# Squares of k summed on GpSimd, sums of q and decoded words in PSUM, a third weight piece and a fifth held group inside S

## The chip, the cores and the metric

One core of a Trainium2 chip runs the whole program. The metric is the device time of one launch in microseconds. TensorE (PE in the profile) multiplies, VectorE (DVE) and ScalarE (ACT) work element by element, GpSimd (POOL) does the same on SBUF only, SyncE (SP) issues most transfers. Each engine runs its own list of instructions in order and waits on semaphores.

## The reference

Three steps follow one another on 6080 tokens. The first is a channel attention: q and k (6080 x 256) are divided by the norm of each column over all tokens, and their product over the tokens is a 256 x 256 matrix S.

```
qn = q / (norm(q, axis=1) + 1e-6);  kn = k / (norm(k, axis=1) + 1e-6)
a  = softmax(kn^T @ qn / tau);      x = (v @ a)
g  = max(0.01 h, h), h = x @ w_in;  x = g @ w_out             # moe
g  = h where h >= 1, 0 where h <= -1, else (h + 1)^2 / 4      # moe2, h = x @ w2_in
out = g @ w2_out
```

All inputs are float32 in value; the four weight matrices (256 x 2048 and 2048 x 256) arrive as 64-bit words, so each weight has two 32-bit halves that the kernel has to join.

## The kernel before

**The stage S.** The tokens come in 15 groups: groups 0 to 3 with two tokens to a partition (256 KB for q, 256 KB for k), groups 4 to 12 with four (512 KB each), group 13 with two, group 14 with two on 96 partitions. Buffers for q and for k turn in rings of six. For a group TensorE adds k^T q into two PSUM banks, `s_ps[0]` and `s_ps[1]`, one for each half of k's columns (L358); a four-token group gives eight products, and each product leaves two rows in the profile. The last `HELD` groups get only the first bank's products in the loop; those for the second bank are kept in a list and issued later by `s_held`: `PRE` (one) right behind the loop, some behind the norm products, the rest behind the first transposes.

**The norms.** ScalarE squares q and k of each group (L376, L379), and VectorE adds the squares to `accq` and `acck`, both in SBUF (L382, L384; folded and finished at L389 and L387). When all groups are in, TensorE sums them over the partitions with a matrix of ones (`nq`, L425; `nk`, L429), ScalarE takes roots (L426, L430), VectorE inverts them (L433 to L436), scales S (L449), takes the maximum (L450), ScalarE the exponential (L451), TensorE turns it (`et_ps`, L456), and a product with the first weights follows (`wps`, L469).

**Weight pieces.** The weights come in 32 pieces of 512 KB (`raw`, three buffers, L144). One piece costs ScalarE a magnitude (L184, `a<-raw`) and VectorE three single-input operations (L197, L199, L206) and three with two inputs (L202, L210, and the last sum L214, L217 or L233); pieces that are used in two parts (high and low) also cost a cast on ScalarE (L224, L241) and a difference on VectorE (L221, L237). This work is a generator, `preparation`, which `pump` and `step` advance from fixed places in the program; ScalarE's parts wait in the list `later` until `flush`, the differences in the list `behind`. `LOAD_AT` names the groups behind whose loads a piece is loaded while S runs. Before, two pieces are decoded inside S and the third around the norms.

**What follows.** The expert layers run as quads (layer, pair of token blocks, slice of the hidden size). The first pair's eight quads, (0, 0, j), use the products wx = (attention times w_in): ScalarE scales them out of PSUM (L721, L519), casts the high part (L722, L524) and VectorE subtracts for the low part (L728 for the second half of j = 0, L527 for each later j). TensorE needs both parts for `ph` (L340, L342). The order of these operations is written out by hand: a list of events with times that only sort them (`PLAN0`, `PUMP`, `FLUSH`, `SUMS`, `HIGHS`, `LOWS`). `SUMS` places four VectorE sums of token blocks for the next pair (L704, `xs`).

## Time and profile before

| | before |
|---|---|
| median of 3 runs (lowest to highest) | 1048.63 us (1048.36 to 1048.72) |
| the profiled execution, its own time | 1048.5 us |
| its span in the trace | 1046.6 us |
| TensorE busy | 1039.6 us (99%) |
| VectorE busy | 815.9 us (78%) |
| ScalarE busy | 835.8 us (80%) |
| GpSimd busy | 20.5 us (2%) |

The profile describes one execution. Times in its rows count from the span's start; the profiled execution's own time is 1.9 us longer than the span, and 0.1 us below the median. A busy share is a mean over stages: TensorE at 99% says that little of the span is left to gain, but its ends are modelled, and rows that stand further apart than their neighbours show where it waited. What ended such a wait stands in brackets behind a row, with the idle time before it.

### The profile page before, as it was taken

The numbers are of one execution on the slowest core, as the hardware profiler recorded it, in microseconds if no ns is written. First come the engines' busy times: TensorE is split into PE (matmuls) and PEld (weight loads), VectorE is DVE, ScalarE is ACT, GpSimd is POOL, SyncE is SP. The second block draws the span as 40 slices with busy tenths as digits, with TensorE's granted clock in tenths as the row PEclk, the third lists the DMA queues.
The fourth block names the chain that finished last, engine by engine and source line by source line (L and its number), as shares of the span: only waits on it lengthen the run. The fifth ranks groups of instructions, "written<-read, shape, count | busy, mean of one in ns | idle before, by whom it ended". The sixth has DMA issues, their size and how long they took to land.

```text
span 1046.6 us, 13454 instructions
## 1 busy us (share of the span) xinstructions
PE 1039.6 (99%) x4656; PEld 868.9 (83%) x4656; DVE 815.9 (78%) x1369; ACT 835.8 (80%) x1436; POOL 20.5 (2%) x36
## 2 busy tenths in 40 slices
PE   9999999999999999999999999999999999999998
PEld 8878888888888888888888888888888888888887
DVE  6999967788787878775557878779778878878765
ACT  6677777777777787777678888888888888888886
POOL 0001100000000000000000000000000000000000
PEclk9999999999999999999999999999999999999999
DMA  9754566468668669557346346446436444543641
GB/s 356 262 191 145 196 227 219 136 214 294 220 208 299 214 215 326 199 190 240 129 155 238 117 166 199 159 139 218 155 123 203 157 162 170 184 150 127 206 140 65
DMA packets 50996, 201.82 MB, mean 193 GB/s; under 512 B 5552, under 2 KB 6576, under 8 KB 50928
## 3 DMA queue, kind: packets, MB, share of 16 engines
q1 hardware_dynamic: 46752, 186.54, 51.0%
q0 software_dynamic: 3888, 14.16, 4.4%
q8 instruction: 37, 0.61, 0.2%
q10 hardware_dynamic: 288, 0.26, 0.1%
q14 instruction: 31, 0.25, 0.1%
HBM read 163.32 MB, written 37.62 MB: 192 GB/s over the span
## 4 chain that ended last, share of the span: by engine, by line
PE 96%; DVE 1%; DMA 1%; issue 0%; ACT 0%; SPq 0%; DVEq 0%
PE acc L342 33%; PE acc L340 16%; PE pX L342 15%; PE pW L342 8%; PE pX L340 8%; PE pW L340 4%; PE pY L342 4%; PE s_ps L358 3%; PE ph L342 2%; PE pY L340 2%; PE ph L340 1%; DMA k<-in_k_dram 1%; PE wps L342 0%; PE wps L469 0%; DVE gl L673 0%
## 5 line engine op out<-in xcount | busy, mean ns | idle before, releaser
L673 DVE TENSOR_TENSOR gl<-c,gh 128x512 fp32r<-128x512 f32 (+1 forms) x384 | 261.1, 680 | 69.8 <-ACT gh L668 69.1
L342 PE MATMUL acc<-gl,l2w 128*128 128x512 f32 (+1 forms) x768 | 297.7, 388 | 0.0
L342 PE MATMUL acc<-gh,l2w 128*128 128x512 f32 (+1 forms) x768 | 297.7, 388 | 0.0
L340 PE MATMUL acc<-gh,l2w 128*128 128x512 f32 (+1 forms) x768 | 297.6, 387 | 0.0
L668 ACT CAST gh<-c 128x512 fp32r<-128x512 f32 (+1 forms) x384 | 234.9, 612 | 5.4 <-DVE c L664 0.8
L342 PE MATMUL pX<-xo,l1w 128*128 128x512 f32 (+1 forms) x704 | 215.6, 387 | 0.0
L342 PEld LDWEIGHTS acc<-gl,l2w 128*128 128x128 f32 x768 | 144.2, 188 | 28.8 <-DVE gl L673 0.2
L342 PEld LDWEIGHTS acc<-gh,l2w 128*128 128x128 f32 x768 | 144.2, 188 | 28.5
L340 PEld LDWEIGHTS acc<-gh,l2w 128*128 128x128 f32 x768 | 144.2, 188 | 28.4
L342 PEld LDWEIGHTS pX<-xo,l1w 128*128 128x128 f32 x704 | 132.2, 188 | 26.2
L655 ACT ACTIVATE u<-c,half 128x512 f32<-128x512 f32 (+1 forms) x144 | 103.8, 721 | 42.4 <-DVE c L641 42.3
L340 PE MATMUL pX<-xo,l1w 128*128 128x512 f32 (+1 forms) x352 | 136.3, 387 | 0.0
L633 ACT COPY s<-pX 128x512 f32<-128x512 f32 (+1 forms) x176 | 101.5, 577 | 30.9 <-PE pX L342 30.9
L658 ACT ACTIVATE u<-u 128x512 f32<-128x512 f32 (+1 forms) x192 | 120.3, 627 | 1.3
L650 ACT ACTIVATE c<-c 128x512 f32<-128x512 f32 (+1 forms) x120 | 75.2, 627 | 56.8 <-DVE c L641 56.5
L342 PE MATMUL pW<-xo,l1w 128*128 128x512 f32 (+1 forms) x352 | 107.8, 387 | 0.0
L641 DVE TENSOR_TENSOR c<-pY,s 128x512 f32<-128x512 f32 (+1 forms) x88 | 60.3, 685 | 60.7 <-PE pY L342 58.7
L664 DVE SCALAR_TENSOR_TENSOR c<-u,c 128x512 f32<-128x512 f32 (+1 forms) x144 | 97.9, 680 | 10.7 <-ACT u L658 10.7
L641 DVE TENSOR_TENSOR c<-pW,s 128x512 f32<-128x512 f32 (+1 forms) x88 | 60.2, 685 | 39.7 <-PE pW L342 28.6
L641 DVE TENSOR_TENSOR c<-pX,s 128x512 f32<-128x512 f32 (+1 forms) x88 | 60.2, 684 | 24.1 <-PE pX L342 20.6
L340 PEld LDWEIGHTS pX<-xo,l1w 128*128 128x128 f32 x352 | 66.1, 188 | 13.1
L342 PEld LDWEIGHTS pW<-xo,l1w 128*128 128x128 f32 x352 | 66.1, 188 | 13.1
(118 smaller groups left out, 1104.3 us busy)
## 6 DMA issues: line engine op xcount, KB each, us to landing
l1w<-l1d SPq DMA_DIRECT2D x80, 896.0 KB, 4.6
l2w<-l2d SPq DMA_DIRECT2D x88, 512.0 KB, 5.2
raw<-in_w_out_dram POOLq DMA_DIRECT2D x14, 512.0 KB, 4.6
l1d<-l1w SPq DMA_DIRECT2D x8, 896.0 KB, 4.3
l1d<-l1s SPq DMA_DIRECT2D x8, 896.0 KB, 4.8
raw<-in_w_in_dram POOLq DMA_DIRECT2D x13, 512.0 KB, 4.4
xr<-in_vT_dram SPq DMA_DIRECT2D x5, 1024.0 KB, 8.4
x<-o SPq DMA_DIRECT2D x20, 256.0 KB, 3.7
```

The source lines that it names most:

```text
L340: nc.tensor.matmul(out=out, lhsT=wh, rhs=mh, start=first, stop=False, skip_group_check=skip)
L342: nc.tensor.matmul(out=out, lhsT=w, rhs=x, start=False, stop=last and w is (wl if late else wh), skip_group_check=skip)
L358: nc.tensor.matmul(out=s_ps[ic], lhsT=kt[:rows, i, ic * P:(ic + 1) * P], rhs=qt[:rows, i, :], start=gi == 0 and i == 0, stop=gi == len(gro ...
L633: A.copy(out=s[i], in_=bank["W" if i == "5" else "X"])
L641: V.tensor_tensor(out=tile_c(r), in0=bank[name], in1=s[i], op=ALU.add)
L650: A.activation(out=c[r], in_=src, func=AF.Prelu, alpha=0.01)
L655: A.activation(out=u[r], in_=source(r), func=AF.Relu, scale=0.5, bias=half[:, 0:1])
L658: A.activation(out=u[r], in_=u[r], func=AF.Square)
L664: V.scalar_tensor_tensor(out=c[r], in0=u[r], scalar=1.0, in1=src, op0=ALU.min, op1=ALU.max)
L668: A.copy(out=g[int(r[0]), int(r[1])][0], in_=c[r])
L673: V.tensor_tensor(out=lo, in0=c[r], in1=hi.bitcast(F32), op=ALU.subtract)
```

## The change

- GpSimd adds the squares of k for groups 2 to 11 into `acck` (`add_k`); VectorE adds those of the last three groups into a new tile `sumk` and then both halves of `acck` to it.
- The sums of q, `accq`, now lie in two PSUM banks and VectorE adds half a group at a time (`add_q`); at group 12 they go over into `sumq` in SBUF.
- The magnitudes and the masked words of the first three pieces lie in PSUM (`psum_words`), and the banks of the norms are taken later (`norm_banks`).
- `LOAD_AT` goes from groups 1 and 5 to groups 3, 6 and 9, so that three pieces are loaded inside S; the fourth goes ahead of the first block of v. A piece may be decoded from the group behind its load on. Group 4 has an extra pump ahead of its squares, and pumping goes on through group 12.
- Five groups are held instead of four; ten held products stand behind the norm products instead of six, five are left behind the first transposes as before.
- Three generator steps around the norms are rearranged, and the four sums of token blocks for the second pair go to later quads.

**The end of S, VectorE.** Before, the sums end with folds and four short adds, and the third piece starts behind them; `rq` (L433) is the first operation of the norms.

```order
L384 TENSOR_TENSOR accq<-accq,sq 128x1024
L389 TENSOR_TENSOR accq<-accq 128x512
L384 TENSOR_TENSOR acck<-acck,sq 128x1024
L389 TENSOR_TENSOR acck<-acck 128x512
L387 TENSOR_TENSOR accq<-accq,sq 128x512
L387 TENSOR_TENSOR acck<-acck,sq 128x512
L387 TENSOR_TENSOR accq<-accq,sq 96x512
L387 TENSOR_TENSOR acck<-acck,sq 96x512
L197 TENSOR_SCALAR a<-a 128x512
L199 TENSOR_SCALAR a<-a 128x512
L433 TENSOR_SCALAR rq<-rq 128x256
```

The same place now, from the third piece's masked words on; ahead of these rows stand its L210, L212 and L215 and the two adds of group 11's squares of q.

```order
L219 TENSOR_SCALAR a<-a 128x512
L223 SCALAR_TENSOR_TENSOR raw<-raw,a 128x512
L375 TENSOR_TENSOR sumq<-accq,sq 128x512
L375 TENSOR_TENSOR sumq<-accq,sumq 128x512
L375 TENSOR_TENSOR sumq<-sumq,sq 128x512
L246 TENSOR_TENSOR a<-a,raw 128x512
L375 TENSOR_TENSOR sumk<-sq 128x512
L375 TENSOR_TENSOR sumq<-sumq,sq 128x512
L375 TENSOR_TENSOR sumk<-sumk,sq 128x512
L375 TENSOR_TENSOR sumk<-sumk,acck 128x512 x2
L375 TENSOR_TENSOR sumq<-sumq,sq 96x512
L375 TENSOR_TENSOR sumk<-sumk,sq 96x512
```

The whole third piece now stands among the last sums and ahead of the last add to `sumq`. ScalarE's list at the same place, before (377, 379, 393 to 407 are the tiles of groups 12, 13 and 14; 417 is the third piece):

```order
L379 ACTIVATE sq_385<-q_377 128x1024
L379 ACTIVATE sq_389<-k_379 128x1024
L379 ACTIVATE sq_399<-q_393 128x512
L379 ACTIVATE sq_402<-k_395 128x512
L379 ACTIVATE sq_411<-q_405 96x512
L379 ACTIVATE sq_414<-k_407 96x512
L184 ACTIVATE a_429<-raw_417 128x512
L426 ACTIVATE rq_432<-nq_161,tiny_125 128x256
```

And now (354, 376, 394 and 413 are the tiles of q of groups 10 to 13; 352 is the third piece):

```order
L424 ACTIVATE sq_366<-k_356 128x1024
L197 ACTIVATE a_371<-raw_352 128x512
L424 ACTIVATE sq_384<-q_376 128x1024
L424 ACTIVATE sq_391<-k_378 128x1024
L424 ACTIVATE sq_402<-q_394 128x1024
L424 ACTIVATE sq_409<-k_396 128x1024
L254 CAST l2w_408<-a_371 128x512
L424 ACTIVATE sq_419<-q_413 128x512
L424 ACTIVATE sq_422<-k_415 128x512
L424 ACTIVATE sq_433<-q_427 96x512
```

The third piece's magnitude moved up behind group 10's square of k, and its cast stands ahead of the squares of groups 13 and 14.

**The first quads, ScalarE**, from the last cast of a token block (`xo`) to the high part of j = 1, before:

```order
L414 CAST xo<-xr 128x512
L721 ACTIVATE w_455<-wps_523,sums 128x256
L722 CAST wx<-w_455 128x256
L184 ACTIVATE a<-raw 128x512
L519 ACTIVATE w_549<-wps_458,sums 128x256
L519 ACTIVATE w_549<-wps_551,sums 128x256
L524 CAST wx<-w_549 128x512
```

And now:

```order
L450 CAST xo<-xr 128x512
L197 ACTIVATE a<-raw 128x512
L237 CAST w1i<-a 128x512
L197 ACTIVATE a<-raw 128x512
L760 ACTIVATE w_479<-wps_549,sums 128x256
L761 CAST wx<-w_479 128x256
L558 ACTIVATE w_572<-wps_482,sums 128x256
L558 ACTIVATE w_572<-wps_574,sums 128x256
L563 CAST wx<-w_572 128x512
```

Two magnitudes and a cast of the fourth piece stand ahead of the scaling of wx. VectorE between the low part of j = 0's second half (L728) and that of j = 1 (L527), before:

```order
L202 SCALAR_TENSOR_TENSOR a<-raw,a 128x512
L728 TENSOR_TENSOR wx<-w_455,wx 128x256
L206 TENSOR_SCALAR e<-a 128x512
L210 SCALAR_TENSOR_TENSOR raw<-raw,e 128x512
L217 TENSOR_TENSOR a<-a,raw 128x512
L197 TENSOR_SCALAR a<-a 128x512
L199 TENSOR_SCALAR a<-a 128x512
L527 TENSOR_TENSOR wx<-w_549,wx 128x512
```

And now (L767 and L566 are the same two low parts):

```order
L210 TENSOR_SCALAR a<-a 128x512
L767 TENSOR_TENSOR wx<-w_479,wx 128x256
L212 TENSOR_SCALAR a<-a 128x512
L234 TENSOR_TENSOR w1i<-a,w1i 128x512
L215 SCALAR_TENSOR_TENSOR a<-raw,a 128x512
L219 TENSOR_SCALAR e<-a 128x512
L223 SCALAR_TENSOR_TENSOR raw<-raw,e 128x512
L246 TENSOR_TENSOR a<-a,raw 128x512
L566 TENSOR_TENSOR wx<-w_572,wx 128x512
```

Six operations stand between the two low parts where five stood, and four of them read two tensors where two did. The diff:

```diff
@@ -22,7 +22,7 @@
 WARM = 8
-HELD = 4
+HELD = 5
 SMALL = 4
@@ -55,7 +55,7 @@
 
-SUMS = [((1, 4.5), (1, 13.6), (2, 4.5), (2, 13.6)), ((1, 5.2), (1, 8.3), (2, 5.2), (2, 8.3)), ((1, 6.0), (1, 9.7), (2, 6.0), (2, 9.7))]
+SUMS = [((1, 4.5), (1, 13.6), (2, 4.5), (2, 13.6)), ((1, 5.2), (1, 8.3), (2, 5.2), (2, 8.3)), ((3, 2.5), (5, 2.5), (5, 9.7), (7, 2.5))]
 HIGHS = [((3, 3.3), (4, 3.3), (5, 3.3), (7, 3.3), (7, 9.4), (7, 12.4), (8, 0.4)),
@@ -64,7 +64,7 @@
 
-LOAD_AT = (1, 5)
+LOAD_AT = (3, 6, 9)
 TAU_AT = 3
@@ -179,8 +179,21 @@
 
+    def psum_words(i):
+        if i == 2:
+            norm_banks()
+        return ps_h.tile([P, 2, 256], F32, tag="h", name="a").bitcast(U32)
+
+    norms = []
+
+    def norm_banks():
+        if not norms:
+            norms.append(ps_h.tile([P, NB], F32, tag="h", name="nq")[:, :C])
+            norms.append(ps_h.tile([P, NB], F32, tag="h", name="nk")[:, :2 * KC].rearrange("p (c t) -> p c t", c=KC))
+        return norms
+
     def magnitude(i):
-        a = started[i] = dec.tile([P, 2, 256], U32, tag="a", name="a", bufs=2)
+        a = started[i] = psum_words(i) if i < len(LOAD_AT) else dec.tile([P, 2, 256], U32, tag="a", name="a", bufs=2)
         A.activation(out=a.bitcast(F32), in_=raws[i][:, :, :, 1].bitcast(F32), func=AF.Abs)
@@ -202,7 +215,7 @@
 
-        e = dec.tile([P, 2, 256], U32, tag="e", name="e")
+        e = psum_words(0) if i < len(LOAD_AT) else dec.tile([P, 2, 256], U32, tag="e", name="e")
         V.tensor_single_scalar(out=e, in_=a, scalar=0xFF800000, op=ALU.bitwise_and)
@@ -249,7 +262,7 @@
                 yield 100
-            while not s_done and (i >= len(raws) or loaded_at[i] + 1 > group[0]):
+            while not s_done and (i >= len(raws) or loaded_at[i] > group[0]):
                 yield 100
@@ -342,14 +355,14 @@
 
-    accs = [ep.tile([P, CPG, C], F32, tag=f"acc{nm}", name=f"acc{nm}", bufs=1) for nm in "qk"]
+    accq = [ps_a.tile([P, NB], F32, tag="acc", name="accq").rearrange("p (i c) -> p i c", c=C) for _ in range(2)]
+    acck = ep.tile([P, CPG, C], F32, tag="acck", name="acck", bufs=1)
+    sumq, sumk = (ep.tile([P, 2, C], F32, tag=f"sum{nm}", name=f"sum{nm}", bufs=1) for nm in "qk")
     s_ps = [ps_a.tile([P, NB], F32, tag="acc", name="s_ps")[:, :C] for _ in range(KC)]
...
 
-    nq = ps_h.tile([P, NB], F32, tag="h", name="nq")[:, :C]
-    nk = ps_h.tile([P, NB], F32, tag="h", name="nk")[:, :2 * KC].rearrange("p (c t) -> p c t", c=KC)
     tiles = []
@@ -357,6 +370,34 @@
                              start=gi == 0 and i == 0, stop=gi == len(groups) - 1 and i == s - 1)
+
+    def add(o, x, y):
+        V.tensor_add(out=o, in0=x, in1=y)
+
+    def add_q(gi, sq, rows):
+        if gi < SMALL:
+            add(accq[gi - 2], accq[gi - 2], sq[:, 0:2, :])
+        elif gi < FOLD - 1:
+            for i in range(2):
+                add(accq[i], accq[i], sq[:, 2 * i:2 * i + 2, :])
+        elif gi < FOLD:
+            add(sumq, accq[0], sq[:, 0:2, :])
+            add(sumq, accq[1], sumq)
+            add(sumq, sumq, sq[:, 2:4, :])
+        else:
+            add(sumq[:rows], sumq[:rows], sq[:rows, 0:2, :])
+
+    def add_k(gi, sq, rows):
+        if gi < FOLD - 1:
+            a = acck[:, 2 * gi - 4:2 * gi - 2, :] if gi < SMALL else acck
+            G.tensor_tensor(out=a, in0=a, in1=sq[:, 0:2, :] if gi < SMALL else sq, op=ALU.add)
+        elif gi < FOLD:
+            add(sumk, sq[:, 0:2, :], sq[:, 2:4, :])
+        else:
+            add(sumk[:rows], sumk[:rows], sq[:rows, 0:2, :])
+        if gi == FOLD:
+            for i in range(2):
+                add(sumk, sumk, acck[:, 2 * i:2 * i + 2, :])
 
@@ -371,31 +412,26 @@
             s_matmuls(1, gi)
-        for t, a in ((qt, accs[0]), (kt, accs[1])):
+        if gi == LOAD_AT[0] + 1:
+            pump(0.1)
+            flush()
+            pump(2.4)
+        for t in tl:
             if gi < 2:
-                A.activation(out=a[:, 2 * gi:2 * gi + 2, :], in_=t[:, :s, :], func=AF.Square)
+                A.activation(out=accq[gi] if t is qt else acck[:, 2 * gi:2 * gi + 2, :], in_=t[:, :s, :], func=AF.Square)
             else:
...
                 A.activation(out=sq[:rows, :s, :], in_=t[:rows, :s, :], func=AF.Square)
-                if gi < SMALL:
-                    h = slice(2 * gi - 4, 2 * gi - 2)
-                    V.tensor_add(out=a[:, h, :], in0=a[:, h, :], in1=sq[:, 0:2, :])
-                elif gi < FOLD:
-                    V.tensor_add(out=a, in0=a, in1=sq)
-                else:
-                    for i in range(0, s, 2):
-                        V.tensor_add(out=a[:rows, 0:2, :], in0=a[:rows, 0:2, :], in1=sq[:rows, i:i + 2, :])
-            if gi == FOLD - 1:
-                V.tensor_add(out=a[:, 0:2, :], in0=a[:, 0:2, :], in1=a[:, 2:4, :])
+                add_q(gi, sq, rows) if t is qt else add_k(gi, sq, rows)
             flush()
-            if gi < len(groups) - 4:
+            if gi < FOLD:
                 pump(S_PUMP[gi > 7])
...
             load_pieces(len(raws) + 1, nc.sync)
-    load_pieces(3, nc.sync)
+    load_pieces(4, nc.sync)
     xr = load_x(0, 0, nc.sync)
@@ -417,24 +453,27 @@
 
-    step(1)
     flush()
     s_held(PRE)
+    nq, nk = norm_banks()
     rq = ep.tile([P, C], F32, tag="rq", name="rq", bufs=1)
     for i in range(2):
-        nc.tensor.matmul(out=nq, lhsT=ones, rhs=accs[0][:, i, :], start=i == 0, stop=i == 1)
+        nc.tensor.matmul(out=nq, lhsT=ones, rhs=sumq[:, i, :], start=i == 0, stop=i == 1)
     A.activation(out=rq, in_=nq, func=AF.Sqrt, bias=tiny[:, 0:1])
...
         for i in range(2):
-            nc.tensor.matmul(out=nk[:, c], lhsT=accs[1][:, i, c * P:(c + 1) * P], rhs=ones[:, :2], start=i == 0, stop=i == 1)
+            nc.tensor.matmul(out=nk[:, c], lhsT=sumk[:, i, c * P:(c + 1) * P], rhs=ones[:, :2], start=i == 0, stop=i == 1)
     A.activation(out=rk, in_=nk[:, :, 0], func=AF.Sqrt, bias=tiny[:, 0:1])
     A.activation(out=dummy, in_=tiny, func=AF.Exp)
-    step(2)
+    while behind:
+        behind.pop(0)()
+    step(1)
+    flush()
     V.tensor_scalar_add(out=rq, in0=rq, scalar1=1e-6)
...
     V.reciprocal(out=rk, in_=rk)
-    s_held(6)
+    s_held(10)
 
...
     wx = {}

```

## Rows read from the trace of the kernel before

**Rows 1.** The page, part 1: busy us (share of span) xinstructions.
```profile
PE 1039.6 (99%) x4656; PEld 868.9 (83%) x4656; DVE 815.9 (78%) x1369; ACT 835.8 (80%) x1436; POOL 20.5 (2%) x36
```

**Rows 2.** TensorE's timeline, S to the transposes: start, us, operation, idle before.
```profile
4.57 4.29 PE L358 MATMUL s_ps<-q,k 128*128 128x256 f32 x16
...
13.45 30.03 PE L358 MATMUL s_ps<-q,k 128*128 128x256 f32 x138 [0.22 <-DMA k<-in_k_dram]
43.31 1.02 PE L425 MATMUL nq<-accq,ones 128*128 128x256 f32 x4
...
44.99 2.84 PE L358 MATMUL s_ps<-q,k 128*128 128x256 f32 x12
49.05 0.41 PE L456 MATMUL et_ps<-ident,e 128*128 128x128 f32 x2 [1.22 <-ACT e L451]
```

**Rows 3.** Windows, TensorE alone: stretch, busy (rows), clock, DMA share, GB/s.
```profile
13.45:43.30 29.85, 29.85 (x138) 1.00 1.03 390
```

**Rows 4.** ScalarE's timeline in S.
```profile
22.50 1.06 ACT L379 ACTIVATE sq<-k 128x1024 f32<-128x1024 f32 x1 [0.23 <-DMA k<-in_k_dram]
23.47 0.67 ACT L184 ACTIVATE a<-raw 128x512 f32<-128x512 f32 x1
...
32.92 1.06 ACT L379 ACTIVATE sq<-q 128x1024 f32<-128x1024 f32 x1 [0.22 <-DMA q<-in_q_dram]
...
41.67 0.68 ACT L184 ACTIVATE a<-raw 128x512 f32<-128x512 f32 x1 [0.41 <-DMA raw<-in_w_out_dram]
```

**Rows 5.** VectorE's groups up to 60 us by shape: count | busy, mean ns.
```profile
L384 DVE TENSOR_TENSOR accq<-accq,sq 128x1024 f32<-128x1024 f32 x9 | 11.0, 1225 | 0.1
...
L199 DVE TENSOR_SCALAR a<-a 128x512 uint32<-128x512 uint32 x5 | 2.1, 427 | 0.2
...
L492 DVE TENSOR_SCALAR w<-wps,sums 128x256 f32<-128x256 f32 x1 | 0.5, 483 | 0.0
...
L433 DVE TENSOR_SCALAR rq<-rq 128x256 f32<-128x256 f32 x1 | 0.3, 293 | 0.7 <-ACT rq L426 0.7
```

**Rows 6.** VectorE's timeline, the last sums.
```profile
41.48 0.68 DVE L387 TENSOR_TENSOR acck<-acck,sq 128x512 f32<-128x512 f32 x1
42.08 0.68 DVE L387 TENSOR_TENSOR accq<-accq,sq 96x512 f32<-96x512 f32 x1
```

**Rows 7.** VectorE's timeline around the first quads.
```profile
49.36 0.69 DVE L210 SCALAR_TENSOR_TENSOR raw<-raw,e 128x512 f32<-128x512 uint32 x1
50.09 0.69 DVE L233 TENSOR_TENSOR a<-a,raw 128x512 f32<-128x512 f32 x1
...
54.08 0.17 DVE L462 RECIPROCAL sums<-sums 128x1 f32<-128x1 f32 x1
...
57.35 0.42 DVE L728 TENSOR_TENSOR wx<-w,wx 128x256 fp32r<-128x256 f32 x1
...
60.27 0.68 DVE L527 TENSOR_TENSOR wx<-w,wx 128x512 fp32r<-128x512 f32 x1
```

**Rows 8.** ScalarE's timeline around the first quads.
```profile
55.45 0.47 ACT L721 ACTIVATE w<-wps,sums 128x256 f32<-128x256 f32 x1 [0.80 <-PE wps L469]
55.95 0.41 ACT L722 CAST wx<-w 128x256 fp32r<-128x256 f32 x1
56.26 0.67 ACT L184 ACTIVATE a<-raw 128x512 f32<-128x512 f32 x1
56.84 0.46 ACT L519 ACTIVATE w<-wps,sums 128x256 f32<-128x256 f32 x1
```

**Rows 9.** TensorE's weight loads, the first of j = 1 for wx.
```profile
61.01 0.19 PEld L342 LDWEIGHTS ph<-xo,wx 128*128 128x128 f32 x1
```

**Rows 10.** TensorE's timeline, the first products of j = 2.
```profile
73.34 0.39 PE L340 MATMUL ph<-xo,wx 128*128 128x512 f32 x1
74.00 0.50 PE L342 MATMUL ph<-xo,wx 128*128 128x512 f32 x1 [0.27 <-DVE wx L527]
```

**Rows 11.** GpSimd's groups up to 3 us.
```profile
masks.py:199 POOL TENSOR_SCALAR_AFFINE_SELECT ident<-ident 128x128 f32<-128x128 f32 x1 | 0.3, 287 | 0.1
```

## The prediction

> **What bounds the kernel now.** I read the page's busy shares first: TensorE has rows over 99% of the span [rows 1], so only stretches where its rows stand apart can give time back. Its timeline over S shows them. The 138 rows from 13.45 follow one another without a gap, 30.03 / 138 = 0.218 us each, up to the norm product `nq` at 43.31; then 12 rows of held products start at 44.99, and the transposes at 49.05 had TensorE idle for 1.22 us, waiting for the exponential [rows 2]. The windows add that the DMA engines are full in the same stretch, share 1.03 at 390 GB/s [rows 3]: S is close to two limits at once. VectorE's list shows a third: its last sums run at 41.48 and 42.08 behind one another without a pause [rows 6], so the sum of q is ready just before `nq` starts. The change touches all three, and the question is which ends last.
>
> **The change part by part.** The profiled execution took 1048.5 us, 0.1 less than the median; I sum against it.
>
> *Loads.* The piece behind group 1 goes behind group 3, still ahead of group 4. The bytes ahead of group 4's k stay the same, so with full DMA engines TensorE's start on it at 13.45, which waited for that k [rows 2], stays: groups 2 and 3 come earlier, and the pause only moves. Value 0. The third piece, 512 KB, now goes ahead of group 10 instead of behind group 14. A four-token load of q or k is 512 KB too, so every load behind it lands one place later: group 10's k where group 11's q landed, at whose landing ScalarE squared it, 32.92; and group 14's k, the last of the same set of bytes, where the third piece landed, at 41.67 less the start of its reader, 41.65 [rows 4].
>
> *Held products.* Four products, eight rows, leave the stream before `nq`: 130 rows from 13.45 would end at 41.7. But the last six (two products of group 14 and the `PRE` one) wait for the landing at 41.65: 41.8 + 6 x 0.218 = 43.1. So TensorE could start `nq` at 43.1 against 43.31. Behind it stand now 20 rows instead of 12. From `nq` to the first held row pass 44.99 - 43.31 = 1.68 us [rows 2], 20 rows take 4.35, so the transposes come 6.03 us behind `nq`; the norm chain alone needed 49.05 - 43.31 = 5.74. The 1.22 us idle is filled, and TensorE itself is late next.
>
> *The sums, where I expect the end to be set.* `nq` waits for the last add to `sumq`, and VectorE's list puts the whole third piece and the adds of `sumk` ahead of it. Group 10's square of k starts at 32.92; the magnitude of the third piece stands behind it, 23.47 - 22.50 = 0.97 later, and takes 0.67 [rows 4]: 34.6. From there VectorE has no pause. An operation that needs the one before it starts 50.09 - 49.36 = 0.73 behind it [rows 7]; one that doesn't, 42.08 - 41.48 = 0.60 [rows 6]. From the first masked operation (L210) to the sum L246 are ten such steps, five of each kind: 5 x 0.73 + 5 x 0.60 = 6.65, so L246 starts at 41.25 and ends at 41.95. On it ScalarE's cast (L254) waits, with the squares of groups 13 and 14 queued behind: 0.58 to the next instruction (56.84 - 56.26 [rows 8]) and 0.67 for each square (the magnitude of the same 512 columns) puts group 13's q at 43.25 and its k at 43.95. VectorE adds them at 43.3 and 44.0, both halves of `acck` at 44.7 and 45.45, the last squares of q at 46.05, done at 46.75. So `nq` starts at 46.8, the transposes at 52.85, 3.8 us later than before, and TensorE is idle 3.7 us ahead of `nq`. **+3.8.**
>
> Ends of that term: I take 0.73 for the three single-input operations on PSUM, which the trace shows only in SBUF, at 0.43 for 512 columns; on PSUM 256 columns took 0.483, against 0.293 in SBUF for 256 [rows 5]. At the SBUF price the three steps shrink by 0.27 each, 0.8 in all; if each of the nine PSUM operations on this path cost another 0.1, it is 0.9 more. So +3.0 to +4.7.
>
> By the Trainium skill, "VectorE: DVE Perf Modes", section "Why PSUM operands drop a tier", any PSUM operand takes a float32 single-input operation from two elements a cycle to one. The 256-column pair agrees; by the rule the sum stands as taken, by the SBUF row it would be 1052.3.
>
> *GpSimd's adds* run beside all this if one of 1024 columns takes less than the loads of a group, 1.05 MB at the 390 GB/s of [rows 3], 2.7 us. The trace has none. Below: VectorE's 1.225 for the same add; above: GpSimd's only row that reads data, 0.287 for 128 columns and one input [rows 11], times eight is 2.3, and twice that for two inputs 4.6. I take 2.3, the plain multiple of its own row. Group 11's k lands two places behind group 10's, at 32.9 + 2.6 or 2.7, its square takes 1.06 [rows 4] and the add 2.3: near 39, long before VectorE wants it at 44.7. Cost 0; I price the other end below. The Trainium skill, "GPSIMD Engine Reference", section 3.1, gives 4497 ns for 2048 columns, so by estimate 2.25 here, and the sum would be the same.
>
> *VectorE's adds of q at half a group each* cost 2 x 0.60 where one of k and one of q cost 2.4 before [rows 5]; up to group 9 they lie in its slack. Cost 0, bound by the tail already summed.
>
> *The first quads.* The fourth piece now stands where the third stood. Everything here is relative to the transposes. VectorE's sum of the fourth piece follows the reciprocal at 54.08 [rows 7]: two two-input operations, so it ends near 54.2 + 0.73 + 0.69 = 55.6. Its cast on ScalarE waits for that, and behind the cast a second magnitude and only then the scaling of wx, 2 x 0.58 later: 56.8, where it stood at 55.45 [rows 8]. Its cast ends at 56.8 + 0.50 + 0.41 = 57.7, so L767 starts 0.35 to 0.4 later than L728's 57.35. From there to the low part of j = 1 VectorE took 60.27 - 57.35 = 2.92 [rows 7]; one single-input operation (0.43 [rows 5]) leaves this stretch, two with two inputs (0.60 to 0.73) come: +0.9. So this low part ends 1.3 later, and TensorE's load of it stood at 61.01 [rows 9], directly behind its end at 60.95: no cover. **+1.3**, between 0.3 (a faster piece) and 1.5.
>
> *Later quads.* VectorE is then about one piece, six operations, ahead, and two of the four token sums leave the stretch before j = 2. There TensorE waited for a late low part: its rows stand 0.66 apart, 0.27 of it idle, and the second takes 0.11 longer [rows 10]. That goes: **-0.5**, between the idle alone and the whole, -0.3 to -0.8. The four sums, 0.6 each, come back in quads 3 to 7, where VectorE by then has no backlog; cost 0, at most 1.
>
> Sum: 1048.5 + 3.8 + 1.3 - 0.5 = 1053.1; with the 0.1 to the median, 1053.2. The likeliest case's own range, all low ends and all high ends a little drawn in: 1050.8 to 1054.6.
>
> **The rivals.**
>
> *The tail is covered (not slower).* If the last add to `sumq` starts by 42.4 instead of 46.05, `nq` goes at 43.1, the transposes at 49.1, and 1.3 - 0.5 remain: 1049.4. The place is the third piece's L210, the price 1 us for each us, and the point of decision is `nq` at 44.6, from where it is over 1050.7. For it: VectorE has less to do in S as a whole. Against it: the list puts 18 operations behind group 10's k, and nothing in it can pass another.
>
> *Also the loads give way (faster).* Without the wait for group 14 and without the late low part, TensorE alone sets the pace: `nq` at 41.75, transposes at 47.8, 1.25 early, and -0.5: 1046.8. Against it: the DMA share of 1.03 and the bytes counted above.
>
> *GpSimd late.* At 4.6 an add, eight of them from 14.5 (group 4's k at 13.45 and its square, 1.06) end at 51.3, `nq` follows two steps of 0.73, one of 0.60 and an end later at about 53.5, 6.7 behind my forecast: 1059.8. It decides from (44.7 - 14.5) / 8 = 3.8 us an add.
>
> *TensorE's clock.* The granted clock is 1.00 in every row here, idle 1.22 us included. At the span's start, after a long idle, 16 rows of S took 4.29 instead of 3.48 [rows 2]. A 3.7 us idle may do the same: at least +0.8, and +6.0 if all 6.03 us behind `nq` ran at half rate; 1054 to 1059, nearest to the row, 1055.
>
> **How the numbers follow.** Forecast 0.66, tail covered 0.16, faster 0.05, GpSimd late 0.06, clock 0.07. A measurement here can tell 0.2%, 2.1 us: below 1046.5 is faster, above 1050.7 slower. Slower is the forecast (nearly all of it), GpSimd and the clock: 0.77. Same is the covered tail and a little of the neighbours: 0.19. Faster 0.04, since that rival mostly stays inside 0.2%. The range leaves out the faster case and the lower part of the covered one, about 0.1, and above it GpSimd and half of the clock, 0.1: 1049.0 to 1055.6.
>
> **What would show it.** Right: in the new trace L246 starts near 41 and the last L375 of 96 rows near 46; TensorE is idle 3 to 4 us before `nq`, with VectorE named as the releaser; no idle before the transposes; about 1 us idle at the first `ph` of j = 1 with L566 named; none at j = 2. GpSimd's adds stand at 2 to 2.6 us and end by 39. Wrong: `nq` near 43 refutes the tail, a releaser on GpSimd the forecast's place, and TensorE's rows at twice their distance behind `nq` would mean the clock.

## The result and the profile after

| | before | after |
|---|---|---|
| median (lowest to highest) | 1048.68 us (1048.36 to 1049.02, 4 runs) | 1055.82 us (1054.79 to 1056.85, 4 runs) |
| profiled execution, its span | 1048.5, 1046.6 us | 1054.79, 1053.0 us |

The change makes the kernel 7.1 us slower, ratio 1.0068 (95%: 1.0055 to 1.008). The prediction said slower by 4.6, 1053.2 us, and its range ended at 1055.6.

TensorE's timeline of the changed kernel, the counterpart of [rows 2] and [rows 10] (start, us, operation, idle before and what ended it):

```profile
12.62 24.41 PE L371 MATMUL s_ps<-q,k 128*128 128x256 f32 x112 [0.39 <-DMA k<-in_k_dram]
...
40.66 1.53 PE L371 MATMUL s_ps<-q,k 96*128 96x256 f32 x6 [0.39 <-DMA k<-in_k_dram]
45.67 1.10 PE L461 MATMUL nq<-sumq,ones 128*128 128x256 f32 x4 [3.47 <-DVE sumq L375]
46.61 1.60 PE L465 MATMUL nk<-ones,sumk 128*128 128x2 f32 x8
48.06 7.26 PE L371 MATMUL s_ps<-q,k 128*128 128x256 f32 x20
55.16 0.38 PE L495 MATMUL et_ps<-ident,e 128*128 128x128 f32 x2
...
68.26 0.73 PE L355 MATMUL ph<-xo,wx 128*128 128x512 f32 x2 [0.83 <-DVE wx L566]
```

Three things are to be seen. `nq` waits 3.47 us for VectorE's `sumq`, as forecast. Behind it the 20 held rows take 7.1 us where 20 x 0.218 = 4.4 were counted. And at j = 1 TensorE waits 0.83 us for L566, while no wait is left at j = 2. The windows, TensorE alone meant, show why the held rows are slow; the columns are stretch, length, busy us of PE, PEld, DVE, ACT and POOL, PEclk, DMA share, GB/s:

```profile
42.20:45.60 3.40, 0.00 (x0) 0.00 (x0) 3.26 (x6) 1.43 (x3) 0.00 (x0) 1.00 0.78 284
46.60:53.30 6.70, 6.70 (x21) 5.64 (x20) 5.40 (x13) 3.38 (x7) 0.00 (x0) 0.51 0.20 81
```

In the idle stretch no row of TensorE stands; in the 6.7 us behind it the granted clock is 0.51, the lower level, 1.2 GHz. VectorE's tail, the counterpart of [rows 6], in its timeline:

```profile
33.58 0.70 DVE L210 TENSOR_SCALAR a<-a 128x512 f32<-128x512 f32 x1 [0.52 <-ACT a L197]
...
40.24 0.69 DVE L246 TENSOR_TENSOR a<-a,raw 128x512 f32<-128x512 f32 x1
...
42.11 0.69 DVE L375 TENSOR_TENSOR sumq<-sumq,sq 128x512 f32<-128x512 f32 x1 [0.59 <-ACT sq L424]
...
43.51 1.42 DVE L375 TENSOR_TENSOR sumk<-sumk,acck 128x512 f32<-128x512 f32 x2
44.84 0.68 DVE L375 TENSOR_TENSOR sumq<-sumq,sq 96x512 f32<-96x512 f32 x1
```

and ScalarE's, the counterpart of [rows 4]:

```profile
31.97 1.06 ACT L424 ACTIVATE sq<-k 128x1024 f32<-128x1024 f32 x1 [0.24 <-DMA k<-in_k_dram]
32.93 0.62 ACT L197 ACTIVATE a<-raw 128x512 f32<-128x512 f32 x1
...
40.96 0.58 ACT L254 CAST l2w<-a 128x512 fp32r<-128x512 f32 x1 [2.72 <-DVE a L246]
41.44 0.63 ACT L424 ACTIVATE sq<-q 128x512 f32<-128x512 f32 x1
```

The chain is the one that the prediction worked out: the third piece's sum L246, the cast that waits for it, the squares behind the cast, the last adds behind the squares. GpSimd's groups show its adds:

```profile
L393 POOL TENSOR_TENSOR acck<-acck,sq 128x1024 f32<-128x1024 f32 x8 | 18.9, 2366 | 8.6 <-ACT sq L424 8.6
```

So the transposes move from 49.05 to 55.16, by 6.11: `nq` is 2.36 later (45.67 - 43.31), and from `nq` to the transposes pass 9.49 us instead of 5.74. The waits at the first quads add 0.83 - 0.27 = 0.56. Together 6.7, where the spans differ by 6.4 (1053.0 - 1046.6) and the profiled executions by 6.3. Of the four executions two stand at a mean clock of 0.997, the profiled one and one of 1055.29 us, and two at 0.995, with 1056.34 and 1056.85. So in those two the clock was low for longer or once more; no trace shows where.

### The profile page after: what moved, and what is told of

Read it like the earlier page. It is cut to its first block, busy times and chain, and to the rows that moved or that the text cites. A ratio compares the mean times of both kernels' runs of the same rounds, so it can differ in the third digit from the quotient of the medians.

```text
span 1053.0 us, 13467 instructions
## 1 busy us (share of the span) xinstructions
PE 1043.2 (99%) x4656; PEld 871.5 (83%) x4656; DVE 809.3 (77%) x1369; ACT 836.6 (79%) x1437; POOL 42.0 (4%) x46
## 4 chain that ended last, share of the span: by engine, by line
PE 94%; DMA 3%; DVE 1%; ACT 0%; issue 0%; SPq 0%; ACTq 0%; DVEq 0%
PE acc L355 33%; PE acc L353 16%; PE pX L355 15%; PE pW L355 8%; PE pX L353 8%; PE pW L353 4%; PE pY L355 4%; PE ph L355 2%; PE pY L353 2%; DMA q<-in_q_dram 1%; DMA k<-in_k_dram 1%; PE ph L353 1%; PE s_ps L371 1%; PE wps L355 1%; DMA wfd<-w 0%; PE wps L353 0%
```

## The experiments

Each was timed beside the kernel before on the same chip; the median of before was 1048.6 to 1048.9 in all of them, so versions from different comparisons are told apart to a few tenths of a us at best. Clocks of single executions are the mean over the whole span.

**TensorE kept busy while it waits.** On the changed kernel:

```diff
+    for _ in range(8):
+        nc.tensor.matmul(out=nq, lhsT=ones, rhs=tiles[FOLD][1][:, 0, :], start=True, stop=True)
     for i in range(2):
         nc.tensor.matmul(out=nq, lhsT=ones, rhs=sumq[:, i, :], ...)
```

> The changed kernel, with eight products whose result is overwritten (16 rows of 128 x 256, about 0.218 us each, 3.5 us) put on TensorE between the last product of S and the norm product nq, so that the 3.47 us that TensorE waits for the last add to sumq are not idle. VectorE's and ScalarE's work stays as it is. Theory A (the idle itself lets the clock fall, and the clock is 2.7 + 0.5 us of the loss): nq still starts at 45.7 (45.3 to 46.2), but the rows behind it stand at 0.11 (nk) and 0.217 us (held products) instead of 0.21 and 0.427, the transposes come at 51.4 to 52.2 instead of 55.16, set by the exponential that is done at 51.3; the time is 1051.3 to 1052.5 us, and its spread is as small as that of the kernel before (0.5 us). Theory B (the rows behind nq are slow for another reason, such as SBUF or PSUM traffic of VectorE, ScalarE or transfers at that place): the rows stay 0.427 us apart, transposes at 55, the time 1054.8 to 1056.9 as before the edit. If the rows are slow from a fall of the clock that any wait for VectorE brings, the result is between: over 1053.

Measured: 1051.70 us (1051.31 to 1052.45, 7 runs), ratio to before 1.0027 (1.0017 to 1.0038). Its TensorE timeline and one window:

```profile
42.13 3.62 PE L461 MATMUL nq<-q,ones 128*128 128x256 f32 x16
45.58 1.11 PE L463 MATMUL nq<-sumq,ones 128*128 128x256 f32 x4
...
47.33 4.56 PE L371 MATMUL s_ps<-q,k 128*128 128x256 f32 x20
51.73 0.38 PE L497 MATMUL et_ps<-ident,e 128*128 128x128 f32 x2
```

```profile
46.60:51.70 5.10, 5.10 (x29) 4.57 (x28) 4.28 (x10) 3.39 (x7) 0.00 (x0) 1.00 0.27 106
```

`nq` starts as late as in the changed kernel, the clock stays at 1.00, and the same 20 rows take 4.4 us. Eight products that compute nothing save 4.1 us (1055.82 - 1051.70; 3.1 between the profiled executions). Theory A holds.

**The same wait without the change.** On the kernel before, eight operations between the last sum of q and `nq`:

```diff
+    for _ in range(8):
+        V.tensor_scalar(out=accs[0][:, 0:2, :], in0=accs[0][:, 0:2, :], scalar1=1.0, scalar2=1.0, op0=ALU.mult, op1=ALU.mult)
```

> The kernel before, with eight operations of VectorE (each 0.43 to 0.47 us, multiplying the finished sums of q by one) put between the last sum and nq: nq starts 3.3 to 3.7 us later, at about 46.8, and nothing else of the change is in it. Theory A (an idle of about 3.5 us of TensorE at this place lets its clock fall, with no part of the change needed): the 12 held rows behind nk stand about 0.43 us apart instead of 0.217, the transposes come at least 4.2 us later than 49.05 (12 rows at half rate end after the exponential is done), the time is 1053.0 to 1055, more than the delay of nq alone. Theory B (the low rate in the changed kernel comes from something that the change adds): the rows stay at 0.217, the transposes come as much later as nq, 52.4 to 52.8, and the time is 1051.9 to 1052.3.

Measured: 1054.20 us (1053.20 to 1055.04, 4 runs), ratio 1.005 (1.0036 to 1.0064); its TensorE:

```profile
10.29 35.17 PE L358 MATMUL s_ps<-q,k 128*128 128x256 f32 x154 [2.18 <-DMA k<-in_k_dram]
47.74 1.38 PE L427 MATMUL nq<-accq,ones 128*128 128x256 f32 x4 [2.28 <-DVE accq L425]
...
50.48 5.22 PE L358 MATMUL s_ps<-q,k 128*128 128x256 f32 x12
55.53 0.38 PE L458 MATMUL et_ps<-ident,e 128*128 128x128 f32 x2
```

The idle was 2.28 us, shorter than planned since S itself ran later, and still the 12 rows stand 0.42 us apart; the windows give the clock of their stretch as 0.50:

```profile
48.90:55.30 6.40, 6.40 (x20) 5.42 (x19) 5.32 (x10) 3.39 (x7) 0.00 (x0) 0.50 0.01 3
```

So the fall needs no part of the change, only the wait. It does not need VectorE either. S ran later because TensorE waited 2.18 us for a landing of k near its start, and from 11.1 to 14.5 us the granted clock was 0.52 there as well. This execution, the slowest of the four, thus has two falls, and its 1055.04 us is not the price of one wait. All four stand at a mean clock of 0.995 to 0.998; where it fell in the other three no trace shows.

**Two pieces in S.**

```diff
-LOAD_AT = (3, 6, 9)
+LOAD_AT = (3, 6)
...
-    load_pieces(4, nc.sync)
+    load_pieces(3, nc.sync)
```

> The changed kernel with only two weight pieces inside S: the third is loaded behind the loop as in the kernel before; everything else of the change stays (sums of k on GpSimd, sums of q in PSUM, five held groups, the order of steps at the norms). Theory A (the third piece's operations on VectorE and ScalarE, ahead of the last sums, set the start of nq): the last add to sumq starts near 42.5 instead of 44.84, nq at 42.9 to 43.4 instead of 45.67, TensorE idle ahead of it under 0.7 us instead of 3.47, all rows behind it at full rate (0.217 us), the transposes at 48.9 to 49.6 instead of 55.16; with the same order at the first quads as in the changed kernel the stall at j = 1 stays near 0.8 to 1.2; the time is 1049.4 us (1048.5 to 1050.5). Theory B (the sums themselves are late: GpSimd's share, the halves in PSUM, or the chain through the folds): nq stays at 45 or later, idle 3 us, rows at half rate, 1054 to 1056.

Measured: 1048.27 us (1047.67 to 1048.69, 11 runs), ratio 0.9996 (0.9987 to 1.0004).

```profile
41.94 1.13 PE L461 MATMUL nq<-sumq,ones 128*128 128x256 f32 x4 [0.49 <-DVE sumq L375]
...
43.71 4.56 PE L371 MATMUL s_ps<-q,k 128*128 128x256 f32 x20
48.11 0.38 PE L495 MATMUL et_ps<-ident,e 128*128 128x128 f32 x2
...
61.21 0.73 PE L355 MATMUL ph<-xo,wx 128*128 128x512 f32 x2 [0.83 <-DVE wx L566]
```

The third piece inside S, with all that follows from it, costs 7.5 us: `nq` is back to 41.94, even ahead of the 43.31 of [rows 2], and the clock stays up. Theory A, though `nq` came 1 us earlier than I expected, and the time 0.2 below its range. The edit does one thing more: `psum_words` goes by the length of `LOAD_AT`, so the third piece's words now lie in SBUF. The next run, which leaves them in PSUM, tells the parts of `nq` apart.

**The third piece loaded in S, decoded behind it.**

```diff
-            if gi < FOLD:
+            if gi < LOAD_AT[2] + 1:
                 pump(S_PUMP[gi > 7])
```

> The changed kernel with the third piece still loaded behind group 9, inside S, but not decoded there: the pumps stop behind group 9, so its six operations on VectorE and its cast on ScalarE come at and behind the norms, as those of the fourth piece in the changed kernel. The magnitude of the third piece is asked for with the rest. This tells the load from the decode. Theory A (the decode's operations ahead of the last sums are the delay; the place of the load costs at most one landing): the last add to sumq starts near 41.2 to 42.5, nq at 41.9 to 43.2 against 45.67, all rows behind it 0.217 us apart, the time within 1 us of that of the kernel with two pieces in S, 1048.3 to 1049.3. Theory B (the third piece's 512 KB among the loads delays the last groups by more than their slack): nq at 44 or later, the wait ahead of it named to a landing of k or q or behind one, time over 1051.

Measured: 1051.27 us (1050.62 to 1052.57, 7 runs). `nq` says what was asked, the total does not:

```profile
43.00 1.13 PE L461 MATMUL nq<-sumq,ones 128*128 128x256 f32 x4 [0.68 <-DVE sumq L375]
...
59.12 0.50 PE L353 MATMUL ph<-xo,wx 128*128 128x512 f32 x1 [2.23 <-DVE l2w L250]
```

Of the 3.73 us by which `nq` is later in the changed kernel than with two pieces, 2.67 (45.67 - 43.00) are the decode and 1.06 (43.00 - 41.94) the place of the load. Each is from one profile, and the second is hardly more than `nq` differs between two kernels with two pieces in S (41.94 here, 42.60 below). The time missed my 1048.3 to 1049.3 since a wait of 2.23 us came up that I had not seen: the profile names the third piece's low part (L250) as what `ph` waits for; as I read it, the piece's words keep a PSUM bank until then, and `ph` needs the bank; no run tries that alone. In this execution the clock stayed at 1.00 behind the wait; three of the seven, at a mean of 0.998, took 1052.5 to 1052.6.

**The three pieces earlier.**

```diff
-LOAD_AT = (3, 6, 9)
+LOAD_AT = (3, 5, 7)
```

> The whole change, with the second and third pieces loaded earlier: behind groups 3, 5 and 7 instead of 3, 6 and 9, so that the third piece's sum stands on VectorE ahead of the folds at group 12 instead of between them and the last adds. Theory A (what costs is only where the third piece stands, since VectorE has idle time of 1 to 2 us ahead of group 10 in the changed kernel): the last add to sumq starts at 41.5 to 42.7, nq at 42.2 to 43.4, no fall of the clock, the transposes at 48.4 to 49.5, and with the stall of 0.83 at j = 1 left and none at j = 2 the time is 1047.8 to 1049.2. Theory B (VectorE cannot hold three pieces and the sums in S at all): nq later than 44.5, idle of 2 us or more, rows behind at half rate, over 1052.

Measured: 1053.26 us (1049.84 to 1054.38, 6 runs). The time and the slow rows are those of theory B, the place of `nq` lies between the two. In the profiled execution, ScalarE and then TensorE:

```profile
34.52 0.59 ACT L254 CAST l2w<-a 128x512 fp32r<-128x512 f32 x1 [1.41 <-DVE a L246]
...
36.91 1.05 ACT L424 ACTIVATE sq<-q 128x1024 f32<-128x1024 f32 x1
```

```profile
44.20 2.04 PE L461 MATMUL nq<-sumq,ones 128*128 128x256 f32 x4 [1.78 <-DVE sumq L375]
```

VectorE's last nine adds run without a pause from 37.98 in that trace, so `nq` gains 1.5 us and not 3. They start late because of ScalarE: the third piece's cast, which waits 1.41 us for L246, stands ahead of the squares of groups 11 and 12, and group 12's q is squared at 36.91, where ScalarE did it at 34.72 with two pieces in S. The piece no longer stands between VectorE's last adds, but it still holds them up through its cast. Two of the six executions, at a mean clock of 1.000, took 1049.8 and 1049.9; the other four, at 0.996 to 0.998, took 1052.8 to 1054.4. One kernel thus shows both, 3 to 4.5 us apart; how long TensorE idled in the executions without a trace is not known.

**The sums of q first.** On the changed kernel VectorE adds acck's halves behind the last adds, and six held products go between `nq` and `nk`:

```diff
-        if gi == FOLD:
+        if gi == FOLD + 1:
             for i in range(2):
                 add(sumk, sumk, acck[:, 2 * i:2 * i + 2, :])
...
+    s_held(6)
     for c in range(KC):
...
-    s_held(10)
+    s_held(4)
```

> The whole change with its loads behind groups 3, 6 and 9, and one order changed on two engines: VectorE adds both halves of acck to sumk behind the last adds instead of ahead of them, and TensorE takes six of the ten held products between nq and nk, since nk now waits longer. Theory A (nq waits only for its place in VectorE's list): two adds of 0.67 us leave the way to the last add to sumq, so nq starts 1.3 us earlier, 44.2 to 44.5, and TensorE's idle ahead of it falls from 3.47 to 2.0 to 2.3 us; since the runs with an idle of 1.78 and 2.28 us at this place still showed rows at half rate, the clock falls in most executions, and the time is 1053 to 1055. If the shorter idle leaves the clock up, nq's 1.3 us and the 2.7 to 3.2 of the slow rows both come back: 1051 to 1052. Theory B (another wait holds nq): no change, 1055 to 1056.

Measured: 1051.77 us (1051.51 to 1054.06, 5 runs). The four executions at a clock of 1.000 took 1051.5 to 1052.3, the profiled one, at 0.998, 1054.06, with `nq` waiting 1.75 us. So the clock did not fall in most, as I had expected, but in one of five. The time of the four is what I had given for a clock that stays up.

**The order at the first quads.** On the changed kernel:

```diff
-    flush()
     wx_part(0, 1)
     w00["plain"]("11")
...
     A.copy(out=wx[0][:, 0, 2:4, :], in_=half_w(w4, 1))
+    flush()
...
-PUMP = [..., ((0.5, 1.4, 3.8), 2.6), ...]
+PUMP = [..., ((0.5, 2.0, 3.8), 2.6), ...]
```

and a magnitude that had been asked for is not asked for again.

> The changed kernel with another order of three operations at the first quads: ScalarE's scaling and cast of the second half of wx for j = 0 stand ahead of the fourth piece's cast and of the next magnitude (which is issued once, not twice), and VectorE's sum of the next piece (0.69 us) stands behind the low part of wx for j = 1 instead of ahead of it. S and the norms are unchanged, so the transposes stay near 55.2. Theory A (the order of these operations makes the low part of j = 1 late): the low part starts 0.9 to 1.2 us earlier counted from the transposes (67.52 - 55.16 = 12.36 in the changed kernel; 11.2 to 11.5 here), TensorE's 0.83 us wait at the first products of j = 1 shrinks to 0.2 or less; the time falls by 0.7 to 1.0 us. Theory B (it is late since VectorE has more to do there, whatever stands first): 0.4 us at most, since the operations that are moved back delay the next ones, and a wait of 0.3 us or more appears at j = 2.

Measured: 1055.76 us (1054.87 to 1056.55, 5 runs), no gain. The low part starts 66.37 - 55.07 = 11.30 behind the transposes, as theory A says, and the wait for it is gone; but another comes up. ScalarE, then TensorE:

```profile
67.69 0.62 ACT L257 CAST l2w<-a 128x512 fp32r<-128x512 f32 x1 [1.11 <-DVE a L249]
68.22 0.61 ACT L710 CAST gh<-c 128x512 fp32r<-128x512 f32 x1
```

```profile
68.98 0.47 PE L356 MATMUL acc<-gh,l2w 128*128 128x512 f32 x1 [0.45 <-ACT gh L710]
```

The sum that I moved back on VectorE has a cast on ScalarE that stands ahead of the cast of gh, and TensorE needs gh next. Neither theory had the wait at this place.

**Two pieces and the whole order mended**: both edits above, and the flush that issues this cast goes behind the cast of gh, which stands at 2.7:

```diff
-FLUSH = [..., (0.4, 2.3, 3.3), ...]
+FLUSH = [..., (0.4, 2.75, 3.3), ...]
```

> The changed kernel with two pieces in S (as in the run with two) and a mended order at the first quads: ScalarE's scaling and cast of the second half of wx for j = 0 ahead of the piece's cast and the next magnitude (issued once); VectorE's sum of the next piece behind the low part of wx for j = 1; and ScalarE's cast that waits for this sum behind the first cast of gh instead of ahead of it. Theory A (the stalls at the first quads come from the order on two queues, and in the run with the first two edits alone the wait moved to the cast of gh since ScalarE stood at a cast that waited for the moved sum): no wait of 0.2 us or more of TensorE at j = 1, neither at the low part of wx nor at gh, and the time is 0.6 to 1.0 us below the run with two pieces, 1047.3 to 1047.7. Theory B (VectorE has too much work there in any order): another wait of 0.4 us or more comes up by 100 us, and the time is 1048.0 to 1048.5.

Measured: 1047.03 us (1046.50 to 1047.51, 11 runs), ratio 0.9985 (0.9976 to 0.9993): 1.5 us faster than the kernel before, 1.24 faster than with two pieces alone, and, with the last version below, the fastest here. Each set against the kernel before beside it, the step from two pieces is 1.04. No wait of TensorE's is left at j = 1 or 2. Theory A, 0.3 below its range. The same mended order with three early pieces:

> Both edits: the three pieces loaded behind groups 3, 5 and 7, and the mended order at the first quads. By the theories A of its two parts the time is that of the earlier loads less 0.6 to 1.0 us: 1047.0 to 1048.3, below the kernel before by 0.5 to 1.7 us. If three pieces in S bring nothing over two, it equals the run with two pieces and the mended order within 0.3 us; if the sums are late with three pieces wherever they stand, it is 1051 or more.

Measured: 1049.20 us (1048.50 to 1052.71, 11 runs); above it, and again with single executions at a clock of 0.997. With the sums of q first as well:

> Three pieces in S, loaded behind groups 3, 5 and 7, the mended order at the first quads, and the same order of the last sums: acck's halves behind the last adds, six held products between nq and nk. Theory A (with the earlier loads nq stood at 44.2 to 44.35, idle 1.76, of which two adds are 1.3): nq at 42.9 to 43.1, idle 0.3 to 0.6, the clock up in all executions, the time 1047.0 to 1048.0, like the kernel with two pieces, and with a spread as small. Theory B (TensorE is late there for another reason): 1048.5 to 1049.5 as without the edit, some executions over 1052.

Measured: 1049.08 us (1048.55 to 1049.95, 11 runs), all at 0.999 or 1.000.

```profile
42.82 1.02 PE L464 MATMUL nq<-sumq,ones 128*128 128x256 f32 x4
...
50.22 0.41 PE L499 MATMUL et_ps<-ident,e 128*128 128x128 f32 x2 [1.16 <-ACT e L494]
```

`nq` no longer waits and the spread is small, as expected, but `nk` behind the held products makes the exponential late, and 1.16 us of idle stand there: the wait moved one step on. The place of `nq` is that of theory A, the time lies in theory B's range, 1.1 above A's.

**GpSimd's part**, on the fastest version:

```diff
-            G.tensor_tensor(out=a, in0=a, in1=..., op=ALU.add)
+            V.tensor_tensor(out=a, in0=a, in1=..., op=ALU.add)
```

> The fastest version so far (two pieces in S, mended order) with the squares of k of groups 2 to 11 summed on VectorE instead of GpSimd, in SBUF, 1.23 us for each of the eight adds of 1024 columns. Theory A (GpSimd's adds carry the gain in S): VectorE was busy for 20.7 of the 27 us from 14 to 41, so another 9 us overfill it; the last add to sumq comes 2 to 4 us later, nq at 44 to 46, the clock falls, time 1050 to 1054. Theory B (VectorE has enough idle time as it had in the kernel before, which did all sums there with two pieces): under 0.7 us of change, 1047.0 to 1047.8.

Measured: 1051.68 us (1048.96 to 1052.94, 8 runs); `nq` at 44.02 behind an idle of 2.59 in the profiled execution. GpSimd's adds are worth 4.6 us here, by the same two steps, a late `nq` and the clock (one execution of eight, at 1.000, took 1048.96). Theory A.

**The fifth held group**, on the fastest version:

```diff
-HELD = 5
+HELD = 4
...
-    s_held(10)
+    s_held(6)
```

> The fastest version so far (two pieces in S, mended order) with four held groups instead of five and six held products behind the norm products instead of ten, as in the kernel before. Theory A (the fifth group fills TensorE's wait for the exponential, which was 1.22 us in the kernel before): TensorE's stream ends 1.7 us later, nq moves from 42.6 to about 43.5 to 44.3, an idle of about 1 us comes back ahead of the transposes, and the time is 0.5 to 1.7 us longer: 1047.5 to 1048.7. Theory B (the fifth group moves work that would be done anyway, as nq waits for the sums): under 0.3 us.

Measured: 1047.18 us (1046.94 to 1047.64, 11 runs), 0.15 from the version with five: theory B. Its trace shows the idle ahead of the transposes back, 1.18 us, and `nq` no later (42.48 against 42.60), in an execution whose S started earlier (12.62 against 14.17). What each of the two is worth cannot be told from one profile each.

## Why the prediction was right in part and wrong in size

- **Late sums, +3.8.** The mechanism, the place and the releaser are right: with the clock kept up the transposes come at 51.73, +2.68, and from L210 to L246 6.66 us passed (40.24 - 33.58) where 6.65 were counted. The term was 1.1 too large, since the chain began about 1 us earlier: group 10's square of k started at 31.97 where I had counted 32.92, and L246 at 40.24 instead of 41.25. The step that failed is that the landings of one execution, TensorE's start at 13.45 first, were taken to stay. S starts at 12.62 here, and group 10's square of k stands at 31.9 to 32.7 in the four other runs with the same loads. What part of that is the change is open: two kernels with the same loads, the versions with five and with four held groups, started S at 14.17 and at 12.62. Single-input operations on PSUM took 0.70 and stood 0.73 apart, the value taken; in SBUF, in the same trace, they took 0.42 to 0.43.
- **The clock, counted at 0: +3.3.** This is what put the time over the range. In the profiled execution `nq` to the transposes took 9.49, with the clock kept up 6.15; between the medians it is 4.1. The step that failed is that the prediction gave the clock 0.07 as a rival to the forecast, by the 1.22 us idle at a clock of 1.00, though its own sum opened an idle of 3.7 us at that place. It was no rival, it was the next term of the same chain, and the trace shows the prediction's own sign for it, rows at twice their distance behind `nq` (0.43 us while the clock is low, 0.22 before). The run with filler products and the one with added operations on the kernel before show it from both sides. Its price was misread too: the 16 rows of 4.29 us do not stand behind an idle but behind 8 warm-up products (16 rows from 1.00 to 4.78), and the granted clock of their stretch is 1.00. That the rival's own 1055 is within 1 us of the median is luck: it has the clock at under 2 us and the late sums 1.1 too large.
- **Held products fill the 1.22 us.** Right: no idle stands ahead of the transposes, and none with the clock kept up. But it was worth nothing that can be measured, as the version with four held groups is as fast.
- **First quads, +1.3 and -0.5.** The low part L566 came 1.14 later, counted from the transposes (67.52 - 55.16 against 60.27 - 49.05). The wait at j = 1 came, with L566 named, at 0.83; the one at j = 2 is gone. Net 0.56 instead of 0.8. Mending the order gave back 1.0 to 1.2 with two pieces.
- **GpSimd.** 2.37 us an add where 2.3 was taken; the last ends at 38.09, hidden. What I put at "cost 0" was right for the cost, but the prediction did not say that without this help the same sums would be late.
- **Rivals.** "GpSimd late" and "tail covered" did not occur. What stays open is why an idle of about 2 us lowers the clock in some executions and not in others.
- **Sums.** Three small ones do not come out as written, and the forecast rests on none. The low ends of the likeliest case add up to 1051.1, so 1050.8 does not draw them in; the covered tail passes 1050.7 from `nq` at 44.4, not 44.6; and "GpSimd late" with two steps of 0.73 gives `nq` at 54.1, not 53.5.

## What to carry to other kernels

When a sum of your own opens an idle on TensorE, look what the trace's granted clock did after other idles, and price the rows behind it at both levels as a part of that sum, not as a separate case. A resource that becomes free early (a bank, a queue, an engine) is not a reason to pull work ahead of the last link of a chain: two pieces beside the sums cost nothing, the third stood in front of the add that everything waited for, and loaded earlier it still held up the squares through its cast. An operation moved on one engine takes its consumers on the next in-order engine with it; look what stands behind them there.

## What the runs showed of the hardware

- TensorE's clock fell to its lower level (0.50 to 0.52) behind much shorter idles than the 3.47 us of the changed kernel, and not by their length alone. In the profiled executions it fell behind idles ahead of `nq` of 2.84 (the run with another order at the first quads), 2.59, 2.28, 1.78, 1.76 and 1.75 us, and behind one of 2.18 us for a landing of k. It stayed at 1.00 behind 2.23 us ahead of `ph`, behind 1.62 us for a landing of k (three early pieces, mended order) and behind the 1.22 us of the kernel before.
- It did not fall in every execution. A mean clock of 0.998 or lower, which does not say where it fell, stands in five of five executions of the kernel with 2.84 us in its profile, in seven of eight with 2.59, four of four with 2.28, three of seven with 2.23, four of six with 1.78, three of eleven with 1.76 and one of five with 1.75. With filler rows in the idle it was 1.000 in seven of seven. In the last comparison two of 24 executions of the kernel before also stood at 0.998, at 1050.4 us, with the median at 1048.89.
- A GpSimd add of two SBUF tensors took 2.37 us at 1024 columns and 1.28 at 512, next to VectorE's 1.23 and 0.69 for the same, and ran beside VectorE and full DMA engines without slowing them: VectorE's two-input operations of 512 columns took 0.68 to 0.70 us with it and without it, and the DMA engines moved 394 GB/s at a share of 1.03, against 390.
